# Gated linear recurrence, then an ELU layer, in fp32: where the carry, the turns and the sums of x's blocks stand in the order of work

## Chip, core and metric

One core of one Trainium2 chip. The metric is the device time of one execution in microseconds. The kernel before took 766.58 us (median of 3 runs, 766.08 to 767.11).

## What is computed

The first stage is a recurrence with a complex decay per position and channel, over 4 batches, 8 heads, 768 positions and 48 channels per head; the second is a dense layer with ELU between two matrices (384 to 2048 to 384), on the 3072 rows that the first one leaves.

```python
mag = np.sqrt(a_re * a_re + a_im * a_im)
scale = np.minimum(mag, 0.999) / (mag + 1e-06)
a_re_n, a_im_n = (a_re * scale, a_im * scale)
for t in range(S):
    new_re = ar * S_re - ai * S_im
    new_im = ar * S_im + ai * S_re
    S_re, S_im = (new_re + kv, new_im)     # kv: outer product of k[t] and v[t]
    y[:, :, t] = np.einsum('bhd,bhde->bhe', q[:, :, t], S_re)
...
h = x @ w_in                               # x: y as rows of 384
g = np.where(h > 0.0, h, alpha * (np.exp(np.minimum(h, 0.0)) - 1.0))
return (g @ w_out).astype(np.float32)
```

## The kernel before

**Units.** The work is cut into 12 units (u = 0 to 11): two batches by 128 positions each, positions on partitions. Units u and u+2 follow each other in time for the same batches. Instead of stepping through time, the kernel sums logarithms of lengths and sums angles over the 128 positions with matmuls by triangular matrices, and then gates q and k by the exponentials and by cosine and sine of these sums.

**The steps of one unit**, each a small function, in this order:

- `squares` (L707): two ScalarE instructions that read the loaded `ar` and `ai`; `joined` (L712) adds them, on GpSimd from u = 4 on. `logarithms`, `powers`, `lengths`, `ratios`, `slopes` and `noted` follow; `angles` (L815) takes the arctangent on ScalarE.
- `carry_back` (L817): a DMA on GpSimd's queue that fetches one row, the last turn of unit u-2. `carried` (L822, instruction at L826) adds this row to the first position's angle, on VectorE. This is "the carry".
- `turns` (L861): for each of the two batches `turned` (L832) sums the angles on TensorE (L837) and takes whole turns off on VectorE (L842, L845); then `carry_on` (L855) sends the last row off with a DMA on GpSimd's queue, for unit u+2.
- `decays` or, from unit 3 on, the first half of the previous unit's `valued` gives the exponentials E and F. `waves` (L959) makes sine and cosine on ScalarE (L970 to L974). `scaled` (L976) multiplies k by F and q by E; `products` (L689) puts k's product on GpSimd from u = 4 on (L984), q's is on VectorE (L985). `ends` (L935) fetches totals with two DMAs on GpSimd's queue (L954). `gated` (L987) multiplies k and q by cosine and sine (L996), k on GpSimd from u = 4 on, q on VectorE.
- `transposed` (L1005) turns gated q and k on TensorE, with copies by ScalarE (L1017). `scored` (L1121), the states (L1057, L1072, L1074) and `valued` (L1145) give the unit's y, which ScalarE copies to x (L1170, L1173). `seam` (L1175) moves parts of y to their place in x with six DMAs on GpSimd's queue (L1183).

**The layer of one unit**, which follows one unit behind:

- `mixed` (L1394, instructions at L1402) makes the sums of x's six blocks of 128 columns: seven VectorE instructions. They wait for the seam's DMAs.
- `mult` (L1428, matmuls at L1434) is one of 20 block products with sums and differences of w_in's blocks, which `summed_in` (L1385) makes once, in the time of the first layers; `kept` (L1447), `joint` (L1450), `low` (L1455, L1456) and `whole_of` (L1459) put the products together and apply the ELU.
- `product(u, k, h)` (L1292, matmuls at L1312) is half of one of seven products P1 to P7 with w_out, taken in the order 1, 4, 2, 5, 6, 7, 3; h is the half. Their results are put together and sent off on VectorE and ScalarE (L1320 to L1334), with two buffers for the output (`o`).

Units 0 to 2 have a layer in another form (`inner`, `elu`, matmuls at L1203), with ScalarE and VectorE emptying three banks of results.

**What sets the order.** Instructions are issued in one program order, and each engine takes its own in that order. For units 0 to 2 and part of 3 that order is the list `first`. The rest are entries `put(at, function, ...)`, where `at` is a due time in slots, 16 slots to a unit; they are sorted by `at`. For unit u, r is 16(u-2): `squares` is due at r+3.4, `carried` at r+17.4, `turns`, `scaled` and `ends` at r+18, `waves` at r+18.5, `gated` at r+19.5, `mixed` of the unit before at the same count r+17.2, and the halves of P7 of the unit before that at r+17.71 and r+18.29, those of P3 at r+18.86 and r+19.43. An entry that stands in `first` is left out of the plan, so the due times of unit 3's carry, turns and gates count for nothing, and its `mixed` counts.

Of the kernel before, what the change touches and what calls it, by code (L numbers as in the profile page):

```python
# [13 lines left out]
ALU = mybir.AluOpType  # L14
# [491 lines left out]
def kernel(  # L506
# [12 lines left out]
    nc = tc.nc  # L519
# [169 lines left out]
    def products(u):  # L689

        return nc.vector if u < 4 else nc.gpsimd

    def new(tag, bufs=1, shape=None):
        return sb.tile(shape or [C, NB, H, D], FP32, tag=tag, bufs=bufs, name=tag)
# [280 lines left out]

    def scaled(u, key=None, n=None):  # L976
        x = nat[u]
        if key is not None:
            by = x["F" if key == "k" else "E"]
            nc.vector.tensor_tensor(  # L980
                out=x[key][:, n], in0=x[key][:, n], in1=by[:, n], op=ALU.mult
            )
            return
        products(u).tensor_tensor(out=x["k"], in0=x["k"], in1=x["F"], op=ALU.mult)  # L984
        nc.vector.tensor_tensor(out=x["q"], in0=x["q"], in1=x["E"], op=ALU.mult)  # L985

    def gated(u, part=None):  # L987
# [14 lines left out]
    PAIRED = 2  # L1002
# [391 lines left out]
    def mixed(u):  # L1394

        x = nat[u]
        b = x["x"].rearrange("p k (n t) -> p (k n) t", n=2)
        six = new("x", 2, [C, NI, GT]).rearrange("p k (n t) -> p (k n) t", n=2)
        lo, hi = halves, pair

        def both(to, a, c, op):
            nc.vector.tensor_tensor(out=to, in0=a, in1=c, op=op)  # L1402

        two = six[:, 0:1].to_broadcast([C, 2, C])
        both(six[:, 0:3], b[:, 0::2], b[:, 1::2], ALU.add)
        both(six[:, 3:5], b[:, 0:2], six[:, 1:3], ALU.add)
        both(hi, two, six[:, 1:3], ALU.add)
        both(lo, b[:, 0:2], b[:, 2::3], ALU.add)
        both(six[:, 5], lo[:, 0], lo[:, 1], ALU.add)
        both(six[:, 0], b[:, 3], b[:, 4], ALU.add)  # L1410
        both(b[:, 2::3], b[:, 2:4], b[:, 4:6], ALU.subtract)
        x["mix"] = {
            0: hi[:, 1], 18: hi[:, 1], 15: hi[:, 0], 9: six[:, 1], 12: six[:, 1], 4: six[:, 2],
            2: six[:, 3], 10: six[:, 4], 16: six[:, 5], 5: six[:, 0], 17: lo[:, 0], 1: lo[:, 1],
            3: lo[:, 1], 19: b[:, 2], 7: b[:, 5], 6: b[:, 3], 8: b[:, 3], 11: b[:, 1],
            13: b[:, 0], 14: b[:, 4],
        }
# [46 lines left out]
    def verdict():  # L1464
# [31 lines left out]
        out=ident, in_=ident, pattern=[[-1, C]], base=0, channel_multiplier=1,  # L1496
# [42 lines left out]
    def put(at, fn, *args):  # L1539
        if fn is hidden:  # L1540
            plan.append((at, len(plan), inner, args))
            plan.append((at, len(plan), elu, args))
        else:
            plan.append((at, len(plan), fn, args))

    def decays_of(u, *at):
        fns = squares, joined, logarithms, powers, lengths, ratios, slopes, noted, angles, carried
        put(at[6] + 0.3, carry_back, u)
        put(at[0], begun, u)
        for x, fn in zip(at, fns):  # L1550
            put(x, fn, u)

    def gates_of(u, *at):
        for x, fn in zip(at, (decays, turns, waves, scaled, ends, gated)):
            if fn is not decays or u <= PAIRED:
                put(x, fn, u)
# [9 lines left out]
        (sums, 0), (warm, 1), (angles, 0, 0), (angles, 0, 1), (summed, 0), (summed, 1),  # L1566
        (decayed, 0, 0), (turned, 0, 0), (decayed, 0, 1), (turned, 0, 1), (waves, 0, 0),
        (waves, 0, 1), (begun, 1), (warm, 1), (scaled, 0, "q", 0), (ends, 0), (scaled, 0, "k", 0),
        (scaled, 0, "k", 1), (scaled, 0, "q", 1), (warm, 1), (gated, 0, 0), (warm, 1), (noted, 0),
        (table, "natural_log"), (warm, 2), (gated, 0, 1), (warm, 2), *3 * [(convert,)],  # L1570
        (transposed, 0, "k", 0), (transposed, 0, "q", 1), (carry_on, 0), (transposed, 0, "q", 0),
# [79 lines left out]
    for u in range(2, NU):  # L1651
        r = (u - 2) * SLOTS
        put(r + (1.5 if u > PAIRED else 8), load_a, u)
        put(r + 8, load_v, u)
        put(r + 8, load_qk, u)
        if u == 2:
            decays_of(u, 16, 16, 17, 17, 18.4, 19.5, 19.6, 22.7, 19.8, 19.8)
            gates_of(u, 20.4, 21.6, 22.1, 22.4, 22.4, 22.6)
        else:
            decays_of(u, r + 3.4, r + 5, r + 12.8, r + 13.2, r + 13.4, r + 13.5, r + 14.9, r + 15.7, r + 15.5, r + 17.4)  # L1660
            gates_of(u, r + 15, r + 18, r + 18.5, r + 18, r + 18, r + 19.5)
        if u > PAIRED:
            for n in range(NB):
                put(r + 22 + 2 * n, transposed, u, "q", n)
                put(r + 23 + 2.3 * n, transposed, u, "k", n)
            at = r + (31.3 if u + 1 < NU else 30.6)
            put(r + 28.2, scored, u)
            put(at, valued, u)
            put(at, seam, u)
            put(r + 33.2, mixed, u)  # L1670
        layer_of(u, r + 36, r + 44)
    for n in range(len(SUMS)):
        put(37 + 0.65 * n, summed_in, n)
# [46 lines left out]
```

## Time and profile before

The page is of one execution of 768.76 us, whose traced span is 767.0 us.

| | us | share of the span |
|---|---|---|
| TensorE matmuls, 7232 | 668.5 | 87% |
| VectorE, 799 instructions | 513.1 | 67% |
| ScalarE, 692 | 428.2 | 56% |
| GpSimd, 193 | 162.7 | 21% |
| sums of x's blocks (L1402): waited for the seam's DMAs | 20.4 in 7 | |
| mean granted TensorE clock | 0.945 of full | |

A profile line of the timeline is: start in us from the span's start, busy us, engine, source line, operation, the tile written and the tiles read, shapes, count; in brackets the idle time of the engine ahead of it and what ended it. PE is TensorE, DVE is VectorE, ACT is ScalarE, POOL is GpSimd, SP issues most loads and stores. Lines that follow each other on an engine can be merged, so a row with a count has the time of them all. Two instructions of one engine overlap a little in the records (the next starts before the last has drained), so the step from start to start is the better measure of a row in a dense stretch.

### The profile page before, as it was taken

The numbers are of one execution on the slowest core, as the hardware profiler recorded it, in microseconds if no ns is written. First come the engines' busy times: TensorE is split into PE (matmuls) and PEld (weight loads), VectorE is DVE, ScalarE is ACT, GpSimd is POOL, SyncE is SP. The second block draws the span as 40 slices with busy tenths as digits, with TensorE's granted clock in tenths as the row PEclk, the third lists the DMA queues.
The fourth block names the chain that finished last, engine by engine and source line by source line (L and its number), as shares of the span: only waits on it lengthen the run. The fifth ranks groups of instructions, "written<-read, shape, count | busy, mean of one in ns | idle before, by whom it ended". The sixth has DMA issues, their size and how long they took to land.

```text
span 767.0 us, 17194 instructions
## 1 busy us (share of the span) xinstructions
PE 668.5 (87%) x7232; PEld 595.5 (78%) x7232; DVE 513.1 (67%) x799; ACT 428.2 (56%) x692; POOL 162.7 (21%) x193
## 2 busy tenths in 40 slices
PE   8898989994995996996996998899699699799995
PEld 6777865673884985995896897799599599699994
DVE  5889997743985486586586576667568458657371
ACT  6865448744472574674575467377277367364150
POOL 2000000220034012511511502503412411501000
PEclk9899999997996999998999899899899899999998
DMA  9985555208013503504423143143250450110000
GB/s 167 173 141 106 149 164 125 54 27 148 15 31 76 95 18 78 120 16 81 91 44 67 44 91 80 44 92 69 43 104 23 85 95 18 48 47 6 23 1 27
DMA packets 151507, 56.12 MB, mean 73 GB/s; under 512 B 129748, under 2 KB 143228, under 8 KB 151420
## 3 DMA queue, kind: packets, MB, share of 16 engines
q1 hardware_dynamic: 147616, 53.58, 34.1%
q0 software_dynamic: 3584, 1.21, 1.4%
q8 instruction: 59, 0.97, 0.6%
q14 instruction: 28, 0.23, 0.1%
q10 hardware_dynamic: 220, 0.14, 0.1%
HBM read 48.91 MB, written 4.81 MB: 70 GB/s over the span
## 4 chain that ended last, share of the span: by engine, by line
PE 48%; DVE 18%; ACT 18%; issue 7%; DMA 5%; POOL 3%; SPq 1%; DVEq 0%; ACTq 0%; POOLq 0%
PE mlp L1312 10%; PE mlp L1434 10%; PE y L1434 5%; PE mlp L1203 5%; DMA x<-y 4%; PE w L1016 4%; PE w L837 3%; ACT n L901 2%; POOL x L1183 2%; PE w L1057 2%; DVE x L1402 2%; PE y L1129 2%; ACT L1456 1%; ACT qt L1017 1%; PE mlp L1228 1%
## 5 line engine op out<-in xcount | busy, mean ns | idle before, releaser
L1312 PE MATMUL mlp<-w_out,g 128*128 128x192 f32 x640 | 123.8, 345 | 12.4 <-DVE o L1333 12.4
L1312 PEld LDWEIGHTS mlp<-w_out,g 128*128 128x128 f32 x640 | 113.1, 203 | 21.2 <-DVE o L1333 15.8
L1074 POOL TENSOR_TENSOR S<-S,T 128x384 f32<-128x384 f32 x36 | 33.5, 931 | 225.7 <-DVE S L1072 225.7
L1203 PE MATMUL mlp<-x,w_in 128*128 128x256 f32 x288 | 68.5, 396 | 12.0 <-DVE g L1214 11.6
L1203 PEld LDWEIGHTS mlp<-x,w_in 128*128 128x128 f32 x288 | 56.3, 199 | 21.9 <-DVE g L1214 12.2
L837 PE MATMUL w<-n,sum_turns 128*128 128x384 f32 x48 | 28.9, 745 | 47.1 <-DVE n L826 46.8
L1459 DVE SCALAR_TENSOR_TENSOR g<-ee,g 128x512 f32<-128x512 f32 x63 | 43.8, 695 | 37.4 <-ACT ee L1456 37.3
L970 ACT ACTIVATE cs<-n 128x768 f32<-128x768 f32 (+1 forms) x14 | 10.5, 751 | 94.8 <-DVE n L845 94.8
L1290 DVE TENSOR_TENSOR g<-g 128x512 f32<-128x512 f32 x80 | 57.6, 732 | 5.7 <-PE mlp L1312 4.7
L1434 PE MATMUL mlp<-x,w_in 128*128 128x128 f32 x432 | 56.4, 277 | 0.9
L1450 DVE TENSOR_TENSOR g<-g,mlp 128x512 f32<-128x512 f32 x45 | 30.7, 683 | 38.0 <-PE mlp L1434 37.2
L837 PEld LDWEIGHTS w<-n,sum_turns 128*128 128x128 f32 x48 | 11.9, 273 | 56.3 <-issue 53.1
L1312 PE MATMUL mlp<-w,g 128*128 128x192 f32 x320 | 54.7, 329 | 0.0
L1434 PEld LDWEIGHTS mlp<-x,w_in 128*128 128x128 f32 x432 | 51.8, 192 | 2.5 <-ACT g L1447 2.5
L1312 PEld LDWEIGHTS mlp<-w,g 128*128 128x128 f32 x320 | 51.8, 190 | 0.7
L1455 ACT ACTIVATE ee<-g 128x512 f32<-128x512 f32 x63 | 39.6, 629 | 19.3 <-DVE g L1450 18.8
L1456 ACT ACTIVATE ee<-ee 128x512 f32<-128x512 f32 x72 | 45.4, 631 | 2.1
L1447 ACT COPY g<-mlp 128x512 f32<-128x512 f32 x36 | 21.2, 589 | 42.3 <-PE mlp L1434 42.3
L1017 ACT COPY qt<-w 128x512 f32<-128x512 f32 x48 | 25.9, 589 | 33.2 <-PE w L1016 33.2
L1183 POOL DMA_DIRECT2D x<-y x62 | 29.8, 487 | 55.9 <-ACT y L1119 37.4
L901 ACT ACTIVATE n<-w 64x384 f32<-64x384 f32 (+1 forms) x60 | 28.1, 486 | 8.9 <-PE w L886 8.3
L996 DVE TENSOR_TENSOR qg<-q,cs 128x1536 f32<-128x1536 f32 (+1 forms) x12 | 31.9, 2661 | 0.0
(216 smaller groups left out, 1476.5 us busy)
## 6 DMA issues: line engine op xcount, KB each, us to landing
w<-in_moe_w_out_dram SPq DMA_DIRECT2D x8, 768.0 KB, 4.3
g<-in_moe_w_in_dram SPq DMA_DIRECT2D x24, 256.0 KB, 2.9
g<-in_moe_w_out_dram SPq DMA_DIRECT2D x24, 256.0 KB
w<-in_moe_w_in_dram SPq DMA_DIRECT2D x16, 288.0 KB, 5.7
vn<-in_v_dram SPq DMA_DIRECT2D x24, 192.0 KB, 4.2
out_dram<-o SPq DMA_DIRECT2D x48, 96.0 KB, 2.8
ar<-in_a_re_dram SPq DMA_DIRECT2D x22, 192.0 KB, 3.6
ai<-in_a_im_dram SPq DMA_DIRECT2D x22, 192.0 KB, 4.8
```

The lines of the kernel that those rows point to most:

```text
L837: nc.tensor.matmul(t, lhsT=sum_turns, rhs=x["th"][:, n].rearrange("p h d -> p (h d)"), start=True, stop=True,)
L901: nc.scalar.activation(out=flat(x[key][to, n : n + 1]), in_=t[of], func=AF.Exp, scale=sign)
L1017: nc.scalar.copy(out=o[:, h0 : h0 + 4], in_=t)
L1074: eng.tensor_tensor(out=new_s, in0=new_s, in1=wide, op=ALU.mult)
L1183: eng.dma_start(out=x["x"][ds(j * HP + D, G), i], in_=x["y"][ds(j * HP + i * G, G)])
L1203: nc.tensor.matmul(t[:, e], lhsT=w_in[:, i, ts(f + e, C)], rhs=x["x"][:, i], start=(i == 0), stop=(i == NI - 1),)
L1290: nc.vector.tensor_tensor(out=S_of(u, k, h), in0=a, in1=b, op=op)
L1312: nc.tensor.matmul(to, lhsT=a[:, m], rhs=b[:, m], start=(first and h == 0 and m == 0), stop=False, skip_group_check=True,)
L1434: nc.tensor.matmul(x["c" + c][:, ts(m, C)], lhsT=a[:, m], rhs=x["mix"][p], start=(p == BANKS[c][0] and m == 0), stop=False, skip_group_che ...
L1455: nc.scalar.activation(out=e, in_=part(u, of), func=AF.Relu, scale=-1.0)
L1456: nc.scalar.activation(out=e, in_=e, func=AF.Exp, scale=-1.0)
L1459: nc.vector.scalar_tensor_tensor(out=part(u, to), in0=nat[u]["e", to], scalar=-1.0, in1=part(u, of), op0=ALU.add, op1=ALU.max,)
```

## The change

From unit 4 on, `carried` is due at r+16.6 (with the products P6 of the layer before) and k's scaling, until now one call with q's, is an entry of its own at r+16.8; `turns` is due at r+18.32, just behind P7's second half, q's scaling at r+18.6, `gated` at r+19.7. `mixed` is due at r+34.45, behind the next unit's turns. Its seven sums stand in another order, and the sum of blocks 3 and 4 is given to GpSimd, where it stands ahead of k's gating. For unit 4 alone, `squares` is due at r+7.2 for r+3.4, and `joined` at r+9.6 for r+5.

In the built program, VectorE has nine instructions fewer and GpSimd nine more (one sum for each of units 3 to 11). On GpSimd's queue the order of a unit is: carry row in, six of the seam, k's scaling, two of `ends`, carry row out, the sum, k's gating, the join of squares; before it was carry row in, six of the seam, carry row out, k's scaling, two of `ends`, k's gating, the join.

```diff
     def scaled(u, key=None, n=None):
         x = nat[u]
+        if n is None and key == "k":
+            products(u).tensor_tensor(out=x["k"], in0=x["k"], in1=x["F"], op=ALU.mult)
+            return
...
-        products(u).tensor_tensor(out=x["k"], in0=x["k"], in1=x["F"], op=ALU.mult)
+        if u <= PAIRED + 1:
+            scaled(u, "k")
         nc.vector.tensor_tensor(out=x["q"], in0=x["q"], in1=x["E"], op=ALU.mult)
...
         both(six[:, 0:3], b[:, 0::2], b[:, 1::2], ALU.add)
+        both(lo, b[:, 0:2], b[:, 2::3], ALU.add)
+        both(hi, two, six[:, 1:3], ALU.add)
+        nc.gpsimd.tensor_tensor(out=six[:, 0], in0=b[:, 3], in1=b[:, 4], op=ALU.add)
+        both(b[:, 2::3], b[:, 2:4], b[:, 4:6], ALU.subtract)
         both(six[:, 3:5], b[:, 0:2], six[:, 1:3], ALU.add)
-        both(hi, two, six[:, 1:3], ALU.add)
-        both(lo, b[:, 0:2], b[:, 2::3], ALU.add)
         both(six[:, 5], lo[:, 0], lo[:, 1], ALU.add)
-        both(six[:, 0], b[:, 3], b[:, 4], ALU.add)
-        both(b[:, 2::3], b[:, 2:4], b[:, 4:6], ALU.subtract)
...
-            decays_of(u, r + 3.4, r + 5, r + 12.8, r + 13.2, r + 13.4, r + 13.5, r + 14.9, r + 15.7, r + 15.5, r + 17.4)
-            gates_of(u, r + 15, r + 18, r + 18.5, r + 18, r + 18, r + 19.5)
+            sq = (r + 7.2, r + 9.6) if u == PAIRED + 2 else (r + 3.4, r + 5)
+            decays_of(u, *sq, r + 12.8, r + 13.2, r + 13.4, r + 13.5, r + 14.9, r + 15.7, r + 15.5, r + 16.6)
+            gates_of(u, r + 15, r + 18.32, r + 18.5, r + 18.6, r + 18, r + 19.7)
+            if u > PAIRED + 1:
+                put(r + 16.8, scaled, u, "k", None)
...
-            put(r + 33.2, mixed, u)
+            put(r + 34.45, mixed, u)
```

In `mixed`, `b` is x as six blocks, `six` a second tile of six blocks, `lo` the tile `halves` and `hi` the tile `pair`.

## Prediction

> **What bounds the kernel now.** I read the waits by engine first, then TensorE's timeline around the largest, then the chain. In the waits each line says who waited for whom, with total us, times, longest.
>
> ```profile
> PE w L837 <- DVE n L826: 46.8, 9, 6.7
> ...
> DVE x L1402 <- DMA x<-y: 20.4, 7, 3.5
> ...
> PE mlp L1312 <- DVE o L1333: 12.4, 10, 3.5
> ...
> PE mlp L1203 <- DVE g L1214: 11.6, 2, 9.5
> ```
>
> TensorE is the engine that fills the span (668.5 of 767.0 us), and these three of its waits hold 71 us. The first returns once per unit, so I take unit 7 (start us, us):
>
> ```profile
> 414.37 1.46 PE L1312 MATMUL mlp<-w_out,g 128*128 128x192 f32 x8
> 421.88 2.90 PE L837 MATMUL w<-n,sum_turns 128*128 128x384 f32 x4 [6.05 <-DVE n L826]
> 424.58 2.70 PE L1312 MATMUL mlp<-w_out,g 128*128 128x192 f32 x8
> 428.12 2.87 PE L1312 MATMUL mlp<-w_out,g 128*128 128x192 f32 x16 [0.84 <-DVE o L1333]
> 430.82 1.05 PE L1434 MATMUL mlp<-x,g 128*128 128x128 f32 x8
> ```
>
> These rows are P7's first half, turns, P7's second half, P3 (both halves), and the first of the next layer's block products. The turns wait 6 us for the carry (L826), and are then slow. The chain says why the carry is late:
>
> ```profile
> 414.03 3.85 DMA x<-y
> ...
> 418.00 0.57 DVE x L1402
> ...
> 420.88 0.87 DVE n L826
> ...
> 421.88 2.90 PE w L837 x4
> ```
>
> VectorE takes its instructions in order: the sums of x's blocks (L1402) stand ahead of the carry and wait for the seam's DMAs. The carry needs neither; its angles end on ScalarE at 413.51, and its row, issued at 410.51, lands in 2.0 us (3.4 at most). So carry and turns pay for somebody else's DMA. From 436 to 475 TensorE is busy 38.3 of 39 us; there is nothing to win there.
>
> One stall stands alone, before the fifth unit:
>
> ```profile
> 182.24 0.84 ACT L709 ACTIVATE n<-ar 128x768 f32<-128x768 f32 x1 [7.98 <-DMA ar<-in_a_re_dram]
> ...
> 187.95 4.63 PE L1203 MATMUL mlp<-x,w_in 128*128 128x256 f32 x12 [9.51 <-DVE g L1214]
> ```
>
> Unit 4's squares block ScalarE until `ar` lands; the first exponentials are queued behind them, and TensorE stands 9.51 us for lack of a free bank.
>
> **The change, part by part.** I call S the start of P7's first half (414.37) and Z the end of the turns' VectorE work (L845; 425.89 before). Mark to mark, I compare the start of the first transposes of q (L1016), behind six block products: S+21.8 in unit 7.
>
> Carry ahead of P7: one VectorE instruction, 0.87 us, now 413.55 to 414.42. Behind it stands P6's sum (414.64 before, waiting for TensorE anyway): at most a tenth later, and nobody waits. Cost nothing, while row and angles stay on time; a late row would move turns only past S+2.8, some 2.4 us off.
>
> Turns behind P7: P7's halves run 1.4 us each, to S+2.8. The carry is long there, so the 6.05 go. The clock comes too. The row for turns without idle time is 156.29: 1.56 us for four; here 2.90, and the half P7 behind them 2.70 against 1.46. That is 2.5 us. VectorE from S+2.85: P7's sum 0.37, two outputs 0.62, turns 0.60+0.47+0.60+0.47: Z = S+6.1. P3 no longer waits 0.84 for its output, as turns lie between. P3 ends at S+2.8+1.5+2.8 = S+7.1.
>
> Sums behind turns: seven operations, 2.55 us (418.00 to 420.55), become six on VectorE: 0.47 (384 columns), four of 0.33, one of 0.21: 2.0. x lands at S+3.5, so the wait of 3.01 vanishes behind turns. The block products need them soon: first none, then `halves` (Z+0.8, block product 2 at Z+1.9), then x's sixth block (Z+1.5). P3's 2.8 us cover this; without P3 the second product would wait until S+6.9 instead of S+5.2, 1.7 us per unit.
>
> The sixth sum on GpSimd: no row shows one of 128 columns. By 0.83 us for 384 columns (L1074) and 1.82 for 768 (L984) it takes 0.3. The Trainium skill, "GPSIMD Engine Reference", "Engine selection", speaks against it: elementwise work belongs on VectorE, GpSimd takes about twice as long. By rule and rows alike it is no saving for the pair of them (0.3 against 0.21); what it can cost depends on SBUF. With both engines free to read at once it saves 0.2; if one shuts the other out, VectorE loses 0.4. I take 0.4; bounds -0.2 and +0.8 (a second collision), eight units. Queued behind it in GpSimd is k's gating, which cannot start before cos/sin: Z+2.79 (unit 11: 665.72 to 668.51). Hidden there.
>
> k's scaling ahead: one instruction of 1.82 us, from 426.76 to behind the seam's DMA issues (414.5), with the two T loads' issues (1.94) behind it; the carry-out DMA (0.48) now follows those, at Z, read two units later. Can it hold up the seam's landing? Units 10 and 11 have no carry-out, so they show this order: k's scaling at 596.21 right behind the seam, sums at 600.15, S+4.1 against S+3.6. Half a us, with 2.0 in hand: nothing.
>
> The port decides what comes next:
>
> ```profile
> 249.85 1.75 DVE L996 TENSOR_TENSOR qg<-q,cs 128x1536 f32<-128x1536 f32 x1
> ...
> 309.98 3.45 POOL L996 TENSOR_TENSOR kg<-k,cs 128x1536 f32<-128x1536 f32 x1
> 310.22 4.83 DVE L996 TENSOR_TENSOR qg<-q,cs 128x1536 f32<-128x1536 f32 x1
> ```
>
> q's gating takes 1.75 alone; begun 0.24 behind k's, it ends 1.62 behind k's end (315.05 against 313.43). It doesn't share, it waits its turn. So sums end at Z+2.4, q's scaling (0.87) at Z+3.3, and k's gating, ready at Z+2.79, starts then, to Z+6.7. q's gating waits for it and ends at Z+8.4 = S+14.5, transposes at S+14.6. TensorE has its six block products (0.89 each) done at S+12.5: a new stall of 2.1 us per unit. The old kernel had it nearly hidden (435.57 against 436.18). Is that stall cold? The Trainium skill, "TensorE: Matmul & The Clock Gate", Part 1: an idle window of some 3.4 us halves the clock. Rows: 3.52 idle, then 5.49 for 16 matmuls of P3; 0.84 idle, then 2.87. Cold by the rule's worst phase, it costs 1.7 us more per unit, 12 us in all; warm, none. 2.1 lies nearer the warm row: I take none.
>
> Gain, from S to transposes (before: units 5 to 11 21.0, 20.9, 21.8, 21.5, 21.3, 21.5, 19.4; after 14.6): 6.4+6.3+7.2+6.9+6.7+6.9+4.8 = 45.2. Unit 4 is different: VectorE has three more summed weights there, and P3 waits 3.52 because k's scaling shuts out L1392 (2.38 for 0.68). It took 26.9; the summed weights and one collision add 3.3 to 14.6: gain 9.0 (10.8 without the collision). The last unit has no turns: its P3 wait of 1.07 goes, its sums are under P3: 0 to 1, I take 0.
>
> Squares later: two ScalarE instructions, 1.6 us, now behind the fourth exponential; `ai` landed at 183.9, so no wait. TensorE wins 9.51, and 1.9 of cold clock (4.63 against 2.76). The join (GpSimd, 1.8) follows into a stretch in which VectorE is busy without a gap (187 to 210) and can shut it out for 1.8; queued behind it are state products a slot or more away. Bounds 9.5 to 11.4, I take 10.
>
> Sum: 45.2+9.0+10 = 64 of the profiled execution's 768.8. The median lies 2.2 lower: 766.6-64 = 702.6, said as 703.
>
> **Rivals.** *The lock falls the other way (0.25):* k's gating gets in ahead of q's scaling (0.4 apart). Then q's scaling, P3's last output and, with the join between, q's gating follow: transposes at S+16.3, block product 4 waits for its bank. Against: six on VectorE are 2.0 us, cos/sin take 2.8. 1.75 more in eight units: 717. If the new stall also turns the clock cold: 729.
>
> *The first stall only moves (0.1):* the join and the squares eat what the loads gave, ScalarE then late for transposes' copies. 10 lost: 713. For: both engines are dense there; against: ScalarE idles 1.25 of every 3.45 us from 192 to 206.
>
> *More is freed (0.1):* k's gating and q's overlap less than I say, the 2.1 goes in half the units: 694.
>
> *Slower (0.05):* the seam's DMAs, with GpSimd and VectorE now at work while they are under way, land late. All sums, and behind them q's scaling and P3's output, queue on VectorE. Slack 2.0 to 2.5; beyond it each us costs eight, so it eats the gain of 64 only from 8 us more: landing about S+14 against S+3.5 to 4.1; landings were 1.6 to 4.7 us. At 15 us late, S+18.6: 703+8 times 12.9 = 806.
>
> *It doesn't do what it says:* built, carry and k's scaling stand ahead of P7, sums and the GpSimd sum as told. Not a rival.
>
> **How the numbers follow.** My sum 0.50, rivals as given. Predicted 703; 0.8 of the chance lies from 692 (rival three and the lower bounds) to 724 (lock, first stall, half of the cold). Within 0.2% (1.5 us, about what a measurement tells from no change) 0.01, all of it out of the case of the late seam, whose other 0.04 are slower; every other case is faster: 0.95.
>
> **What would show it.** The wait of L837 for L826 falls from 46.8 to under 3 us, turns take 1.5 us behind P7; the DMA wait of the sums is gone; a wait of TensorE's L1016 for q's gating of about 2 us in most units is new, q's gating shows 3.5 to 5 us; squares no longer wait 7.98. A period of 54 us for 60.5. Wrong: turns still waiting (row or angles late), sums waiting for the seam, or a clock below full in the middle of units.

## The result, and the profile after

The changed kernel takes 701.8 us (median of 4 runs, 700.64 to 702.24) against 766.85 for the kernel before on the same chip (4 runs): ratio 0.915, 95% interval 0.913 to 0.917. The profiled execution took 702.24 us, its span is 700.4 us for 767.0 before, TensorE is busy 652.6 us of it, and the mean granted clock is 0.983 for 0.945. One run of one experiment kernel (732.0 us, the kernel with the turns in front and all sums on VectorE), more than 1.5% above the fastest of its kernel, is left out of its numbers below.

TensorE's waits, in the same columns as before (who waited for whom, total us, times, longest):

```profile
PE w L1020 <- DVE qg L1000: 11.2, 8, 1.7
...
PE mlp L1316 <- DVE o L1337: 2.8, 3, 1.1
PE w L837 <- DVE n L826: 2.7, 2, 1.6
```

The wait for the carry has gone from 46.8 to 2.7 us, and what is left of it belongs to units 3 and 4. A new one stands at the top: the transposes wait for q's gating, 1.4 to 1.7 us in most units. The sums of x's blocks (now L1406) wait for no DMA any more.

TensorE's timeline around the turns of unit 7:

```profile
385.11 2.76 PE L1316 MATMUL mlp<-w_out,g 128*128 128x192 f32 x16
387.71 1.45 PE L837 MATMUL w<-n,sum_turns 128*128 128x384 f32 x4
389.00 2.76 PE L1316 MATMUL mlp<-w_out,g 128*128 128x192 f32 x16
391.60 1.05 PE L1438 MATMUL mlp<-x,g 128*128 128x128 f32 x8
...
399.17 1.09 PE L1020 MATMUL w<-ident,qg 128*128 128x128 f32 x8 [1.51 <-DVE qg L1000]
```

Both halves of P7 are one row, the turns stand behind them without a wait and at full speed, P3 and the block products follow without a gap. From P7's start (S) to the first transposes of q it is 14.06 us, for 21.81 before (the changed kernel's units 5 to 11 all lie between 14.04 and 14.07). The whole unit takes 53.1 us for 60.9.

VectorE and GpSimd in the same stretch, first VectorE:

```profile
392.08 1.02 DVE L1406 TENSOR_TENSOR x<-x 128x256 f32<-128x256 f32 x2
...
393.23 0.94 DVE L989 TENSOR_TENSOR q<-q,n 128x768 f32<-128x768 f32 x1
...
394.37 4.75 DVE L1000 TENSOR_TENSOR qg<-q,cs 128x1536 f32<-128x1536 f32 x1
```

```profile
385.55 1.82 POOL L979 TENSOR_TENSOR k<-k,n 128x768 f32<-128x768 f32 x1
...
392.30 0.52 POOL L1412 TENSOR_TENSOR x<-x 128x128 f32<-128x128 f32 x1 [0.47 <-DVE pair L1406]
393.75 3.75 POOL L1000 TENSOR_TENSOR kg<-k,cs 128x1536 f32<-128x1536 f32 x1 [0.92 <-POOL x L1412]
```

GpSimd's sum runs at 392.30. Of VectorE's two sums beside it, one row here, the second takes 0.68 us, where one of its size takes 0.42. k's gating is ready at 393.75 while q is still scaled (to 394.10), works from there to 397.5, and q's gating, 1.75 us long when it is alone, shows 4.75: it waits for k's.

Where the 66.6 us of the span lie, by the first transposes of q of each unit:

| stretch | before | after | difference |
|---|---|---|---|
| up to unit 3 | 177.35 | 177.97 | +0.6 |
| unit 4 | 77.47 | 61.29 | -16.2 |
| units 5 to 11, seven steps | 420.75 | 372.15 | -48.6 |
| behind unit 11 | 91.43 | 88.99 | -2.4 |

The first and the last row are no effect of the change that these runs could show: over the 14 profiled kernels of this study the start up to unit 3, whose code is the same in all, ended between 174.5 and 182.4, and the end took 89.0 to 91.4, also in kernels that do not touch it. In the last row TensorE's last matmul ends 82.8 us behind the mark for 83.0 before; the rest is the last output on VectorE, which in the trace before waited for an earlier store to land. For this reason the steps of the units are compared below, beside the medians. Medians are put on one scale as ratio times 766.85.

### The profile page after: what moved, and what is told of

It is laid out like the page before. It is cut to its first block, busy times and chain, and to the rows that moved or that the text cites. A ratio compares the mean times of both kernels' runs of the same rounds, so it can differ in the third digit from the quotient of the medians.

```text
span 700.4 us, 17232 instructions
## 1 busy us (share of the span) xinstructions
PE 652.6 (93%) x7232; PEld 586.1 (84%) x7232; DVE 519.8 (74%) x790; ACT 426.6 (61%) x692; POOL 172.9 (25%) x202
## 4 chain that ended last, share of the span: by engine, by line
PE 45%; DVE 27%; ACT 19%; issue 6%; DMA 1%; ACTq 1%; POOL 0%; DVEq 0%; POOLq 0%
PE mlp L1316 16%; PE mlp L1438 6%; DVE qg L1000 5%; PE y L1438 5%; PE w L1020 4%; PE w L1061 3%; PE mlp L1207 3%; PE y L1106 3%; PE y L1133 2%; ACT L1460 1%; ACT L735 1%; ACT qt L1021 1%; DVE g L1454 1%; ACT ee L1460 1%; DVE n L842 1%
## 5 line engine op out<-in xcount | busy, mean ns | idle before, releaser
L1316 PE MATMUL mlp<-w_out,g 128*128 128x192 f32 x640 | 115.0, 331 | 3.0 <-DVE o L1337 2.8
L1316 PEld LDWEIGHTS mlp<-w_out,g 128*128 128x128 f32 x640 | 105.5, 192 | 7.1 <-DVE o L1337 5.1
L1294 DVE TENSOR_TENSOR g<-g 128x512 f32<-128x512 f32 x80 | 59.2, 751 | 5.7 <-PE mlp L1316 4.6
L1438 PE MATMUL mlp<-x,w_in 128*128 128x128 f32 x432 | 58.5, 279 | 4.1 <-DVE o L1337 3.4
L970 ACT ACTIVATE cs<-n 128x768 f32<-128x768 f32 (+1 forms) x14 | 10.5, 751 | 54.8 <-DVE n L845 54.8
L1000 DVE TENSOR_TENSOR qg<-q,cs 128x1536 f32<-128x1536 f32 (+1 forms) x12 | 40.4, 3367 | 0.0
L1020 PE MATMUL w<-ident,qg 128*128 128x128 f32 x192 | 26.6, 285 | 11.4 <-DVE qg L1000 11.2
L820 POOL DMA_DIRECT2D n<-carry x10 | 5.4, 538 | 121.9 <-DVE n L780 67.3
L1020 PEld LDWEIGHTS w<-ident,qg 128*128 128x128 f32 x192 | 22.7, 147 | 14.2 <-DVE qg L1000 13.7
```

The source lines that it names most:

```text
L1000: eng.tensor_tensor(out=to[:, :, :, 0:D], in0=each.unsqueeze(2).to_broadcast([C, step * H, 2, D]), in1=x["cs"][:, n * H : (n + step) * H], ...
L1020: nc.tensor.transpose(t[:, h], of, ident)
L1294: nc.vector.tensor_tensor(out=S_of(u, k, h), in0=a, in1=b, op=op)
L1316: nc.tensor.matmul(to, lhsT=a[:, m], rhs=b[:, m], start=(first and h == 0 and m == 0), stop=False, skip_group_check=True,)
L1438: nc.tensor.matmul(x["c" + c][:, ts(m, C)], lhsT=a[:, m], rhs=x["mix"][p], start=(p == BANKS[c][0] and m == 0), stop=False, skip_group_che ...
```

## Experiments

My theory after the result was simple: the order of work does it. With the sums behind the turns the carry is early, and the other parts give little. Its rivals were that GpSimd's part of the order (k's scaling, the sum, the loads) carries much of it, and that the squares give less than told.

### The sums alone, on the kernel before

```diff
-            put(r + 33.2, mixed, u)
+            put(r + 34.45, mixed, u)
```

> The kernel before with one number changed: the sums of x's blocks due at r+34.45 instead of r+33.2 (all seven on VectorE, in their old order; carry, turns, squares and k's scaling as before). Theory (the gain is the order alone: the carry no longer stands behind a wait for the seam's DMAs): the turns' wait of 46 us is gone, transposes of q at about S+14.8 against S+14.06 after and S+21.3 before; units 4 to 11 win 45 to 52 us, 715 to 722. Rival A (the turns have to stand behind P7, or P3 waits for the outputs as long as it saves): 735 to 745. Rival B (k's scaling ahead is what frees the gates): 740 to 755.

Measured: 764.4 us, ratio 0.993 (0.990 to 0.996). The theory fell. The turns no longer wait (0.49 us in unit 7), but TensorE then stands at the second block product:

```profile
430.44 2.07 PE L1434 MATMUL mlp<-halves,g 128*128 128x128 f32 x8 [5.38 <-DVE halves L1402]
```

It waits for the sum `halves`, and the row of the sums on VectorE says why; below it GpSimd's queue in the same stretch:

```profile
421.44 8.28 DVE L1402 TENSOR_TENSOR x<-x 128x384 f32<-128x384 f32 x2
```

```profile
420.52 1.84 POOL L984 TENSOR_TENSOR k<-k,n 128x768 f32<-128x768 f32 x1
422.29 1.94 POOL L954 DMA_DIRECT2D T<-ends  x2
424.24 3.44 POOL L996 TENSOR_TENSOR kg<-k,cs 128x1536 f32<-128x1536 f32 x1
427.63 1.80 POOL L716 TENSOR_TENSOR n<-n 128x768 f32<-128x768 f32 x1
```

Two sums that take 1.0 us without company (before, 418.00: 1.02) take 8.28. The first ends at 422.8, just behind k's scaling; the second, begun at 422.82, ends at 429.72, just behind the join. The late sums have met GpSimd's work, and the stall of 6 us has only moved. So moving the sums is not enough: GpSimd has to be out of their way.

### What of GpSimd's queue holds them

First the two T loads (`ends`, L954, which fetch totals into the tile T), put behind k's gating:

```diff
-            gates_of(u, r + 15, r + 18, r + 18.5, r + 18, r + 18, r + 19.5)
+            gates_of(u, r + 15, r + 18, r + 18.5, r + 18, r + 19.6, r + 19.5)
...
-            put(r + 33.2, mixed, u)
+            put(r + 34.45, mixed, u)
```

> The kernel before with the sums at r+34.45 and the two T loads at r+19.6, behind k's gating on GpSimd's queue. Theory (a VectorE sum that begins under the T loads' issues is passed by k's gating and the join; without them it gets the port after k's gating at the latest): the wait of block product 2 falls from 5.4 to about 3 us, 742 to 752. Rival (k's scaling and gating alone hold the sums up): 762 to 767.

Measured: 763.69 us, 0.996 (0.993 to 0.9995). The rival held: moving the loads gains nothing. The sums are held as before, one after the other:

```profile
420.52 4.94 DVE L1402 TENSOR_TENSOR x<-x 128x384 f32<-128x384 f32 x2
425.38 2.02 DVE L1402 TENSOR_TENSOR pair<-x 128x256 f32<-128x256 f32 x1
427.32 2.02 DVE L1402 TENSOR_TENSOR halves<-x 128x256 f32<-128x256 f32 x1
```

GpSimd here gates k until 425.17, issues the loads until 427.04 and joins until 429.05; a sum ends 0.3 to 0.4 us behind each of the three. So the loads hold a sum at their new place too, and what they alone cost is not shown.

Then k's scaling, taken out of the way by an entry of its own ahead of P7, as the change does; carry, turns, squares and the sums' own order stay as before:

```diff
+        if n is None and key == "k":
+            products(u).tensor_tensor(out=x["k"], in0=x["k"], in1=x["F"], op=ALU.mult)
+            return
...
-        products(u).tensor_tensor(out=x["k"], in0=x["k"], in1=x["F"], op=ALU.mult)
+        if u <= PAIRED + 1:
+            scaled(u, "k")
...
+            if u > PAIRED + 1:
+                put(r + 16.8, scaled, u, "k", None)
...
-            put(r + 33.2, mixed, u)
+            put(r + 34.45, mixed, u)
```

> The kernel before with the sums' due time moved to r+34.45, as in the first experiment (0.993 of the time before), and with k's scaling as its own entry ahead of P7 (r+16.8); carry, turns, squares and the sums' own order stay as before. Theory: in the first experiment GpSimd's queue (k's scaling, two T loads, k's gating, join, one behind the other from the end of the turns' work) is what holds VectorE's sums up; with k's scaling gone from there, only k's gating and the join stand against them, and three sums pass before k's gating begins. The kernel with turns ahead of P7's second half and all sums on VectorE took 721.5 on the scale of 766.85 before, with the squares worth 6.3; without those 728, and up to 8 us more because `halves`, which the second block product needs, stands fifth in the old order of sums and is the one held up: 728 to 740. Rival: k's scaling alone does little without the sums' new order and the early carry, since k's gating still stands in front of `halves`: 750 to 764.

Measured: 749.73 us, 0.979 (0.973 to 0.984), 750.4 on the common scale. That is 11 us below the sums alone, but 10 above the end of the theory's range, where the rival's begins. k's scaling was one part of what holds the sums; TensorE's timeline of unit 7 shows the others:

```profile
409.28 1.53 PE L837 MATMUL w<-n,sum_turns 128*128 128x384 f32 x4 [1.47 <-DVE n L826]
...
413.98 2.87 PE L1316 MATMUL mlp<-w_out,g 128*128 128x192 f32 x16 [1.87 <-DVE o L1337]
...
419.10 1.16 PE L1438 MATMUL mlp<-halves,g 128*128 128x128 f32 x8 [1.36 <-DVE halves L1406]
421.45 2.05 PE L1438 MATMUL mlp<-x,w_in 128*128 128x128 f32 x16 [1.19 <-DVE x L1406]
```

The carry, left behind P7's start, now meets k's scaling (406.49 to 408.31) and takes 1.92 us on VectorE for 0.93 in the first experiment; P3 waits for the output that stands behind the turns' work and q's scaling; `halves`, fourth in the old order of the sums (not fifth, as the expectation says), begins at 415.37, behind the start of k's gating at 415.15, and takes 3.68 us. Each of these is what another part of the change removes: the carry's place, the turns' and q's scaling's place, the sums' order.

### The turns back in front of P7's second half

```diff
-            gates_of(u, r + 15, r + 18.32, r + 18.5, r + 18.6, r + 18, r + 19.7)
+            gates_of(u, r + 15, r + 18, r + 18.5, r + 18, r + 18, r + 19.5)
```

This is the changed kernel with turns, q's scaling and gating at their old due times; everything else of the change stays.

> The changed kernel with turns, q's scaling and gating back at r+18, r+18 and r+19.5: turns ahead of P7's second half, carry-out ahead of the two T loads on GpSimd's queue; carry, k's scaling, sums and GpSimd's sum stay as changed. The first run showed VectorE's sums stuck for 7 to 8 us while GpSimd went from the T loads' issues through k's gating to the join. Theory (GpSimd's sum needs VectorE's, so k's gating cannot pass the sums; VectorE gets the port at the latest when GpSimd comes to its sum): transposes at S+14 to S+14.6, 702 to 707. Rival (the T loads under the sums are enough to hold VectorE up for several us): 720 to 745.

Measured: 714.02 us, 0.932 (0.927 to 0.936), 13 us above the changed kernel: more than I told, less than the rival. The mechanism is one I had left out. q's scaling (0.95 us) and the turns' work now stand in front of P7's sum and its outputs on VectorE, and P3 waits 1.87 us in unit 7 for its output buffer (16.7 us in ten waits for 2.8 in three):

```profile
392.80 2.87 PE L1316 MATMUL mlp<-w_out,g 128*128 128x192 f32 x16 [1.87 <-DVE o L1337]
...
398.87 1.16 PE L1438 MATMUL mlp<-x,w_in 128*128 128x128 f32 x8 [0.53 <-DVE o L1337]
```

S to transposes is 15.0 for 14.06: the waits of 1.87 and 0.53 are new, and the 1.51 for q's gating is gone. The carry is early, so from unit 5 on the turns themselves wait in neither place; what the place behind P7 gains is P3's wait.

### GpSimd's sum on VectorE, with the turns in either place

```diff
-        nc.gpsimd.tensor_tensor(out=six[:, 0], in0=b[:, 3], in1=b[:, 4], op=ALU.add)
+        both(six[:, 0], b[:, 3], b[:, 4], ALU.add)
```

With the rest of the change as it is:

> The changed kernel with the sum of blocks 3 and 4 on VectorE, at its new place in the order. Theory (GpSimd's 0.52 us shuts VectorE out for 0.35, VectorE would need 0.21): the sums end 0.1 us earlier, q's scaling still starts ahead of k's gating, 701 to 702, no difference. Rival (GpSimd's sum is what keeps k's gating behind q's scaling): the port falls the other way, 1.75 us per unit, 714 to 716.

Measured: 700.88 us, 0.912 (0.910 to 0.915), no difference from the changed kernel; S to transposes 14.12 for 14.06. With the turns back in front as well:

> As the run before, with the sum of blocks 3 and 4 on VectorE. Theory (without GpSimd's sum ahead of it k's gating passes the sums, and with it the join): block product 2 waits for the sums, transposes at S+15.5 to S+17.3, 714 to 728. Rival (GpSimd's sum is no guard, as it made no difference with the turns behind P7): as the run before, within 2 us.

Measured: 720.92 us (three runs), 0.941 (0.935 to 0.947), 7 us above the kernel with the turns in front and the sum on GpSimd, as expected. Here the place of the sum matters. On GpSimd's queue k's gating stands behind the sum, and the sum waits for `pair`, so k's gating cannot start before VectorE has made three of its sums, and the sum's own time lets two more through: only the last is held (3.54 us in unit 7), and TensorE waits only the 0.53 us shown above for the output that stands behind it. Without the guard k's gating starts at 400.35, the next three sums take 5.71 us together, and TensorE waits for them:

```profile
405.99 2.05 PE L1438 MATMUL mlp<-x,w_in 128*128 128x128 f32 x16 [2.16 <-DVE x L1406]
```

With the turns behind P7 the guard is not needed. k's gating begins 2.8 us behind the turns' VectorE work (Z) in either place, as it waits for cosine and sine; but the sums begin at Z, not 1.8 us behind it, since q's scaling and the outputs no longer stand between, and are done (392.23) before k's gating begins (392.62). As it stands, the GpSimd sum is neither a cost nor a gain.

### k's scaling back beside q's

```diff
-                put(r + 16.8, scaled, u, "k", None)
+                put(r + 18.6, scaled, u, "k", None)
```

> The changed kernel with k's scaling due with q's at r+18.6, behind the turns and GpSimd's sum. Theory: k's scaling (1.8 us) then stands between GpSimd's sum and k's gating and holds the port against q's scaling or waits for it; k's gating starts 1 to 2 us later than Z+3.2, q's gating and the transposes follow, eight units: 710 to 718. Rival (k's scaling is hidden wherever it stands, since k's gating waits for cosine and sine): 702 to 704.

Measured: 716.35 us, 0.932 (0.929 to 0.935). The theory held. VectorE's last sum takes 1.91 us for 0.28, as k's scaling (402.47, 1.99 us) starts first; counted from S, k's gating starts 1.1 us later than in the changed kernel and q's ends 1.6 later. S to transposes is 15.68, 1.6 more than in the changed kernel, and the units' steps are 54.5 to 55.7 for 52.8 to 53.4. So k's early scaling is worth some 13 us even with everything else in place. TensorE's rows show two waits close together:

```profile
405.81 1.16 PE L1438 MATMUL mlp<-x,w_in 128*128 128x128 f32 x8 [1.68 <-DVE o L1337]
...
410.47 1.09 PE L1020 MATMUL w<-ident,qg 128*128 128x128 f32 x8 [1.72 <-DVE qg L1000]
```

Behind the second the granted clock is 0.50 from 412 to 415 us; in the changed kernel, with one wait of 1.51, it stays at 1.00.

### The squares of the fifth unit

Back to their old place in the changed kernel, and moved alone in the kernel before:

```diff
-            sq = (r + 7.2, r + 9.6) if u == PAIRED + 2 else (r + 3.4, r + 5)
+            sq = (r + 3.4, r + 5)
```

> The changed kernel with unit 4's squares and join at their old due times. By the prediction's step (10 us): 712. By what the trace after shows (TensorE 11 us earlier at the first product, but only 5.9 us at P7, since VectorE is 2 us later and TensorE then waits 2.41 us for it and runs at half clock): 707 to 709. If the squares did nothing: 702.

```diff
-            decays_of(u, r + 3.4, r + 5, r + 12.8, ...
+            decays_of(u, *((r + 7.2, r + 9.6) if u == PAIRED + 2 else (r + 3.4, r + 5)), r + 12.8, ...
```

> The kernel before with unit 4's squares and join alone at the new due times. By the prediction's step: 10 us less, 757. By the trace after (VectorE, without a gap in that stretch, can follow only by 9 us, and TensorE then waits 2.4 us for it and is cold): 6 to 8 us less, 759 to 761.

Measured: 708.77 us (0.925, 0.921 to 0.929), some 8 above the changed kernel, and 759.92 us (0.992, 0.990 to 0.994), 6.3 below the kernel before. By the medians that is 6 to 8 us; the steps of unit 4 say 7.3 (68.57 for 61.29) and 8.7 (68.80 for 77.47). The sum had 10, and the second pair's interval (4.6 to 7.9) excludes its lower bound of 9.5. Where the rest went is to be seen in TensorE's rows of the changed kernel, behind the place of the old stall:

```profile
202.21 1.94 PE L1061 MATMUL w<-vn,kg 64*64 64x48 f32 x60 [2.41 <-DVE S L1076]
204.08 2.93 PE L1316 MATMUL mlp<-w_out,g 128*128 128x192 f32 x8
206.80 3.72 PE L1316 MATMUL mlp<-wt,g 128*128 128x192 f32 x16
```

in the same rows of the kernel before:

```profile
210.76 1.13 PE L1057 MATMUL w<-vn,kg 64*64 64x48 f32 x60 [0.56 <-DVE S L1072]
211.82 1.57 PE L1312 MATMUL mlp<-w_out,g 128*128 128x192 f32 x8
213.23 2.76 PE L1312 MATMUL mlp<-wt,g 128*128 128x192 f32 x16
```

and in the changed kernel's table by stretches (busy us of PE, PEld, DVE, ACT and POOL with counts, then the granted clock, the DMA share and GB/s):

```profile
202.20:204.00 1.80, 1.79 (x60) 1.78 (x60) 1.46 (x3) 0.00 (x0) 1.03 (x2) 0.50 0.03 9
204.00:207.00 3.00, 3.00 (x13) 2.92 (x10) 2.06 (x5) 0.00 (x0) 2.16 (x3) 0.50 0.00 0
...
399.00:402.00 3.00, 2.83 (x24) 2.71 (x25) 1.72 (x4) 2.13 (x4) 1.80 (x1) 1.00 0.28 87
```

TensorE reaches its first product with w_out 10.5 us earlier (194.89 for 205.40), but VectorE, which works there without a gap, reaches the state's sum (L1076, 201.60 for 210.16) only 8.6 earlier. TensorE waits 2.41 us for it where it waited 0.56, and the clock falls to half: the three rows take 3.1 us more than before. 1.85 and 3.1 of the 11.1 won (10.5 and the 0.6 of the later start) are given back.

Was it the join, which shuts VectorE out while it works on GpSimd? In the changed kernel, for unit 4 alone:

```diff
-            products(u).tensor_tensor(out=x["m2"], in0=x["m2"], in1=x["sq"], op=ALU.add)
+            (nc.vector if u == PAIRED + 2 else products(u)).tensor_tensor(out=x["m2"], in0=x["m2"], in1=x["sq"], op=ALU.add)
```

> The changed kernel with unit 4's join of squares on VectorE (0.95 us) instead of GpSimd (2.33 us in the trace after, VectorE's fold beside it 2.92 for 1.42). Theory (the squares' gain is eaten by the join that shuts VectorE out): VectorE 0.5 us earlier, TensorE's 2.41 us wait for it falls to about 1.9, and the half clock behind it may go: 0.5 to 3.5 us, 698 to 701. Rival (VectorE has no slack there whatever stands in it): 701.5 to 702.5.

Measured: 701.78 us, 0.913 (0.909 to 0.917): no difference, and TensorE still waits 2.3 us for the state's sum. So it is not the join's engine that costs the time; that VectorE has no slack in this stretch fits its rows, which follow each other without a gap.

### The pair of gatings

The new stall comes from q's gating, which waits for k's. Two ways to let q in earlier. k's gating as two GpSimd instructions of half the size, from unit 4 on:

```diff
-            eng.tensor_tensor(
-                out=to[:, :, :, 0:D], in0=each.unsqueeze(2).to_broadcast([C, step * H, 2, D]),
-                in1=x["cs"][:, n * H : (n + step) * H], op=ALU.mult,
-            )
+            cuts = 2 if key == "k" and u > PAIRED + 1 else 1
+            for m in range(0, step * H, step * H // cuts):
+                here = slice(m, m + step * H // cuts)
+                eng.tensor_tensor(
+                    out=to[:, here, :, 0:D],
+                    in0=each[:, here].unsqueeze(2).to_broadcast([C, step * H // cuts, 2, D]),
+                    in1=x["cs"][:, n * H : (n + step) * H][:, here], op=ALU.mult,
+                )
```

> The changed kernel with k's gating from unit 4 on cut into two instructions, one per batch. Theory (the rest of TensorE's stall, 1.4 to 1.5 us per unit, and another half us in the block products' place, is q's gating shut out by k's): q's gating gets the port after the first half, ends 1.7 us earlier, stall gone in units 4 to 11: 689 to 692. Rival (GpSimd takes the port for both halves in one go): 702. Rival (the stall is a wait for q's scaling or for the output buffer): 701 to 703.

Measured: 689.98 us, 0.898 (0.895 to 0.901), as expected. In unit 7, GpSimd first:

```profile
391.61 5.41 POOL L1003 TENSOR_TENSOR kg<-k,cs 128x768 f32<-128x768 f32 x2 [0.93 <-POOL x L1416]
```

```profile
392.23 3.11 DVE L1003 TENSOR_TENSOR qg<-q,cs 128x1536 f32<-128x1536 f32 x1
```

q's gating ends at 395.34, between the end of k's first half (393.72) and that of the second (397.02), and the stall at the transposes is gone (S to transposes 12.4). And q's gating first, with a GpSimd copy of one element of gated q in front of k's gating, so that k's cannot start before it:

```diff
+    mark = cst.tile([1, 1], FP32, name="mark")
...
-        for key in ("k", "q") if part is None else ("q", "k"):
+        for key in ("k", "q") if part is None and u <= PAIRED + 1 else ("q", "k"):
...
+            if key == "k" and u > PAIRED + 1:
+                nc.gpsimd.tensor_copy(out=mark, in_=gates["q"][0:1, NB - 1, H - 1, 1, D - 1 : D])
```

> The changed kernel with q's gating first and, on GpSimd, a copy of one element of gated q ahead of k's gating, so that k's gating starts behind q's (the copy's target is read by nobody). Theory (the port): q's gating takes 1.75 us alone and ends at Z+5.2, ahead of the block products; k's gating ends at Z+8.9, just ahead of k's first transposes: stall gone, 687 to 691. Rival (the stall moves to k's transposes): 698 to 703.

Measured: 684.6 us, 0.892 (0.889 to 0.895), the fastest kernel of the study and 2.4 us below what I told. VectorE's row of q's gating in unit 7, and TensorE's transposes:

```profile
386.13 1.74 DVE L1003 TENSOR_TENSOR qg<-q,cs 128x1536 f32<-128x1536 f32 x1
```

```profile
389.26 1.04 PE L1023 MATMUL w<-ident,qg 128*128 128x128 f32 x8
```

q's gating takes its 1.74 us, k's begins at 388.08 and takes 3.46, and nobody waits: k's transposes stand two block products later, at 391.92. S to transposes is again 12.4, and from unit 5 on the two kernels' steps are alike (51.1 to 52.6 in both). Of the 6.4 us between their profiled spans 1.5 lie in unit 4 and 4.5 ahead of unit 3's transposes, where no edit is. By the units' steps the two ways are about equal, apart from unit 4. But the medians lie 5.4 us apart and the runs of the two kernels do not overlap (687.92 to 692.21 and 683.62 to 685.69), so a difference that stands in every run is not excluded; its cause is not shown.

## Why the prediction was right, and where it was not

The time told was 703 and it is 701.8. Step by step:

**Carry and turns: right.** Carry ahead of P7 cost nothing (L826 at 384.27, and the wait for it 2.7 us in all), the turns stand at S+2.6 (told S+2.8) and take 1.45 us (told 1.56), and the clock came back with them: in the page's slices it is 0.9 or more from 210 to 683 us.

**Sums and GpSimd's sum: right in sum.** Z, the end of the turns' VectorE work, is S+5.84 (told 6.1), the sums end 2.28 later (told 2.4). GpSimd's sum takes 0.52 and not 0.3, beside VectorE's sum, and holds VectorE's next sum up by 0.26, for the 0.4 that I took. Whether it is there makes no difference, as two kernels show. The prediction missed what it could be good for, a guard in front of k's gating; with the turns behind P7 the guard is not needed.

**k's scaling: right that it costs nothing.** The seam landed in time, no sum waited for it. But the prediction treated its place as free and no more. Held back to q's scaling it costs 13 us, and in the kernel before with late sums its place is worth 11.

**The port: right.** q's scaling came ahead of k's gating in all eight units, by 0.5 us, but in unit 4 by no more than 0.2 (233.31 against 233.50); I told 0.4. In unit 7 k's gating ended at Z+6.5 (told 6.7), q's at Z+8.2 (told 8.4), and the transposes followed at S+14.06 (told 14.6). The stall is 1.5 us for 2.1, and warm: the row in the table by stretches has clock 1.00 right behind it. That part was in some measure luck: stalls of 1.7 to 2.4 us went cold in some places of these runs (the last section has a count), so "nearer the warm row" was no safe ground for the 2.1 us told; in most units the stall that came was shorter than any of these. Here the Trainium skill, "SBUF — State Buffer", "Who interferes with whom", gives the reason: a VectorE instruction with two inputs in SBUF contends with a GpSimd instruction that reads SBUF, the pair of ports that they share is an exclusive lock, and the order of issue decides who blocks. The rows agree here (1.75 us alone, 4.75 behind k's 3.75), and the last experiment turned the rule to use; where the rows do not follow the order of issue is told in the last section.

**Units 5 to 11: told 45.2, measured 48.6.** The term was undersized by 0.5 us a unit, which is about what the stall fell short of its 2.1 us. **Unit 4's window: told 9.0, measured 9.6** (from S to the transposes 26.86 and 17.24).

**Squares: wrong in size.** Told 10, with 9.5 to 11.4 as bounds; the unit's step shows 6.6, the medians of the experiments 6 to 8. The step that failed is the pair of bounds. It took TensorE's stall and its cold clock as won, and asked of VectorE's gapless stretch only whether it would shut the join out. It did not ask who waits for VectorE there. TensorE, let go early, ran into the state's sum. Rival two had this in kind (the first stall only moves), though with another cause, ScalarE late for the copies, and for the whole of the 10.

**Last unit: told 0.** Its P3 still waits, 0.84 us for 1.07, and TensorE's last matmul ends 0.2 us earlier. The other 2.2 of the end are a store's landing, within what other kernels show there.

So the sum of 64 met the 66.6 of the span because 3.4 us too few in the units and 3.4 too many in the squares cancelled; unit 4's 0.6 and what scatters at the two ends make the rest. The time was right partly by that luck.

**The rivals.** The lock did not fall the other way, the stall did not go cold, the seam was not late. What was wrong in my thinking came after the result: that the order of the sums alone was the change. The first experiment gave 5 us where that theory told some 50. On the common scale the steps from before to after, as these kernels have them: sums late 5; k's scaling ahead 11; carry ahead, sums reordered and squares later together 29 (the squares alone 6); GpSimd's sum with the turns still in front 7; turns and q's scaling behind P7 13. Together 65. The carry's place and the new order of the sums were not separated, so how their 23 us divide is not shown. Each of these is the worth of a part in this order of adding; in another order it differs, as GpSimd's sum shows, worth 7 in one place and nothing in the other.

## What to carry to other kernels

A wait that is moved along a queue is won only if the moved work finds its engine, and its port, free at the new place: look up what the other engine that shares the port does at that time, before pricing the move. Where two engines exclude each other, the one whose result is needed first should start first, and a small operation that depends on it, put in front of the other's, is enough to enforce it; here that was worth some 14 us by the units' steps and 17 by the medians. When a stall is priced at its full length, ask which wait of the same engine is next, and on whom.

## What the runs showed of the hardware

- A VectorE operation held by GpSimd does not always come next. In the changed kernel q's gating ran ahead of the join, as soon as k's gating had ended; with the sums alone moved, one sum of 256 columns (0.42 us alone) was passed by two loads' issues, k's gating and the join, and took 6.90 us. In the kernel with the loads later, a sum stood from 425.38 to 427.40 while GpSimd only issued DMAs, directly behind its gating; in the kernel with turns in front and the sum on VectorE, sums under the same issues (398.44 to 400.33) took their usual 0.42 us. What decides this was not settled.
- An operation on one partition is held too: the carry (a row of 768) took 1.92 us beside k's scaling for 0.93.
- The clock fell to 0.50 behind an idle time of 2.41 us, and stayed there for some 6 us of full work, while the stalls of 1.5 us left it at 1.00. The Trainium skill, "TensorE: Matmul & The Clock Gate", Part 1, tells of some 3.4 us of idle time; here less was enough. A count over all 14 traces says how much: the changes of the granted clock in a trace lie whole multiples of 3.41 us apart. Cut into stretches of this length, from 60 us to 10 us before the end, all 72 falls to 0.50 come right behind a stretch in which TensorE had no matmul at work for 1.72 us or more, and none of the 2502 stretches at full clock without a fall behind them had more than 1.93. So in these runs about half a stretch was enough, and whether a wait of 2 us was cold hung on where it lay. In the first 60 us falls also come behind stretches with as little as 0.27 us idle; what decides there is not shown.
- The same code up to unit 3's transposes took 174.5 to 182.4 us in 14 profiled executions, more than several of the effects looked for.
